# A small-h branch of h - tanh(h) rewritten: tanh times a squared arctan in place of a polynomial times tanh

## The chip, the cores and the metric

The kernel runs on one core of a Trainium2 chip. The core has a matrix engine (TensorE, "PE" in the profile), a vector engine (VectorE, DVE), a scalar engine for functions of one operand (ScalarE, ACT), a general engine (GpSimd, POOL) and a queue engine (SyncE, SP); each works through its own list of instructions in order and waits on semaphores of the others. [...] The metric is the device time of one execution in microseconds (us), as the median of several runs. Beside it stands one profiled execution with a record of every instruction.

## The reference

An attention with a decaying state (four batches, eight heads, 768 steps, 48 numbers a head), and a dense block behind it, which is what the change touches:

```python
for t in range(S):
    cur = einsum('bhd,bhe->bhde', u * k[t], v[t])
    y[t] = einsum('bhd,bhde->bhe', r[t], state + cur)
    state = w * state + einsum('bhd,bhe->bhde', k[t], v[t])
x = y.transpose(0, 2, 1, 3).reshape(3072, 384)
h = x @ w_in                 # 384 -> 2048
g = h - np.tanh(h)
out = g @ w_out              # 2048 -> 384
```

For small h the difference h - tanh(h) is about h cubed over three, and two numbers nearly alike are subtracted. So a kernel needs a second formula there, and a choice between the two for each element.

## The kernel before

**Units.** The attention is worked off in units of 64 steps of two batches. A unit loads r, k and v, transposes r and k on PE (L810), scales them on VectorE (L814, or L834 and L835 in later units), multiplies in 64 x 64 blocks (L760), writes diagonal blocks on ScalarE (L858), masks on VectorE (L993), updates the state (L951, L1002), and evicts its rows into `xt`, the input of the dense block (L924, with a part by DMA at L945).

**Weights.** The weights arrive as 64-bit numbers and are converted on the chip, in sixteen pieces of 768 columns: two steps on ScalarE (L141, L142) and five on VectorE (L139, L140, L143, L144, L145) for each piece. A dense tile can't begin before its piece is converted.

**Dense tiles.** There are 96 tiles: 256 tokens by 256 of the 2048 inner columns. For each, PE makes h in PSUM with twelve matmuls (L171). Two buffers of h take turns, so the matmuls of the tile after next wait until `s`, `th`, `tg` and `g` of this one have read it (L1053). ScalarE takes five steps (`act`, L175 to L188): `s` is the square of h, `th` is tanh h, `tg` is tanh of G1 times h, `q` is the square of (s + M1), and `small` is relu(SMALL - s), above zero where h is small. VectorE takes four (`vec`, L190 to L201): `g` = h - th; `c1` multiplies tg by C4 times s; `c2` multiplies it by (q + K1); `cp` copies tg over g where `small` isn't zero. `q` and `small` both read `s`, `c1` reads `s`, and `c2` reads `q`. The finished g goes to PE: for the first 24 tiles and for the very last as o = g times w_out, eight matmuls (L209), otherwise as seven products in place of eight (L260), for which GpSimd builds sums of g (L245 to L249) and VectorE gathers the results (L288).

**The order.** Nothing is scheduled by hand or by the framework: `lay_out` gives each step to a planner as a task with an engine, a modelled cost and the tasks that it comes after (`add`, in `hidden` from L1044 for the dense tiles). `Plan.order` works out due times backward and forward, and then tries seeded random shifts of them (`moved`), 2500 on the first 240 modelled microseconds and 500 on all, and keeps each that doesn't lengthen the modelled span. `Plan.follow` takes over the due times of the first 90 us from a plan of a simpler layout, and searches 500 times behind that. The instructions are then written out in the order of the plan. So a task that goes, or an edge that moves, alters the order of all engines. Where PE has a gap at the start, the planner puts matmuls of the identity into it (`fills`, L688). A first ACTIVATE at L726 brings ScalarE's function tables in.

Of the kernel before, what the change touches and what calls it, by code (L numbers as in the profile page):

```python
# [18 lines left out]

SMALL = 0.25
G1 = 1.0046999454498291
C4 = 0.0015550695700212612
M1, K1 = -6.776710510253906, 167.42614473500566

# [119 lines left out]
class Dense:  # L148


    def __init__(self, nc, work, gpool, ps_d, shared, out, rows, outs=None, last=None, seven=None, parts=None):
        self.nc, self.work, self.gpool, self.ps_d, self.new_outs, self.seven = nc, work, gpool, ps_d, outs, seven
        self.parts = parts
        self.out, self.rows, self.xts, self.sums, self.last, self.negative = out, rows, {}, {}, last, set()
        self.d, self.w_in_sb, self.w_out_sb, self.m1b, self.smallb = (
            shared[x] for x in ("dims", "w_in", "w_out", "m1b", "smallb"))

    def tile(self, j, fs, f):

# [14 lines left out]

    def act(self, t, x):  # L175
        A = self.nc.scalar
        out = self.tmp(x)
        setattr(t, x, out)
        if x == "s":
            A.activation(out, t.h, AF.Square)  # L180
        elif x == "th":
            A.activation(out, t.h, AF.Tanh)  # L182
        elif x == "tg":
            A.activation(out, t.h, AF.Tanh, scale=G1)  # L184
        elif x == "q":
            A.activation(out, t.s, AF.Square, bias=self.m1b)  # L186
        else:
            A.activation(out, t.s, AF.Relu, bias=self.smallb, scale=-1.0)  # L188

    def vec(self, t, x):  # L190
        V = self.nc.vector
        if x == "g":
            t.g2 = self.gpool.tile([128, 2, self.d.NT], F32, name="g", tag="g")
            t.g = t.g2.rearrange("p z t -> p (z t)")
            V.tensor_tensor(t.g, t.h, t.th, ALU.subtract)  # L195
        elif x == "c1":
            V.scalar_tensor_tensor(t.tg, t.s, C4, t.tg, ALU.mult, ALU.mult)  # L197
        elif x == "c2":
            V.scalar_tensor_tensor(t.tg, t.q, K1, t.tg, ALU.add, ALU.mult)  # L199
        else:  # L200
            V.copy_predicated(t.g, t.small.bitcast(I32), t.tg)  # L201

# [95 lines left out]
        queue.dma_start(out=self.out[runs[z] : runs[z] + size, :], in_=o[z * size : (z + 1) * size])  # L298


ACT_STEPS, VEC_STEPS = ("s", "th", "tg", "q", "small"), ("g", "c1", "c2", "cp")


class Plan:
# [243 lines left out]
def near(ctx, tc, r, k, v, w, u, out, shared, moe_w_in, moe_w_out):  # L548
# [145 lines left out]
    def lay_out(early, across_by):  # L694
# [3 lines left out]
        def add(*args, **more):  # L698
            return plan.add(*args, **more)
# [23 lines left out]
            out=ub.rearrange("p h d -> p (h d)"),  # L723
            in_=bass.AP(tensor=u.tensor, offset=u.offset, ap=[[0, 128], [1, H * D]])), data=.7)

        add("ACT", 1.3, lambda: A.activation(fixed("warm", [128, 1]), shared["one"], AF.Tanh), due=0)  # L726


        def steps(generator):
# [313 lines left out]

        def hidden(j, fs, f, due, pace, seven=False):  # L1044
            t = dense.tile(j, fs, f)
            none = SimpleNamespace(g=None, c1=None, c2=None, cp=None, o=None, h=None, s=None, q=None, small=None, th=None, tg=None, empty=[], emptied=[])
            m = len(tiles)
            plan.at = "tile", j, f
            b1, b2, b3, b5 = (tiles[m - i] if m >= i else none for i in (1, 2, 3, 5))
            x = SimpleNamespace(empty=[], emptied=[])  # L1050
            tiles.append(x)
            piece = f // 4 * 4 + f // 2 % 2
            now = add("PE", 1.29, lambda: dense.h(t, 0), filled[j, "all"] + [converted[piece], b1.h, b2.s, b2.th, b2.tg, b2.g] + ([flagged] if m == 1 else []), due, steps=12)  # L1053
            x.h = add("PE", 1.29, lambda: dense.h(t, 1), [now], due + 1.3, steps=12)
            last_h[j] = x.h
            if m == 0:
                plan.fills.append(([], now, fills(idle)))
            x.s = add("ACT", .48, lambda: dense.act(t, "s"), [x.h, b2.c1, b2.q, b2.small, b1.s])
            x.th = add("ACT", .48, lambda: dense.act(t, "th"), [x.h, b2.g, b1.th] + ([units[m].rk, units[m].kw] if m < L else []))
            x.tg = add("ACT", .48, lambda: dense.act(t, "tg"), [x.h, b2.cp, b1.tg])  # L1060
            x.q = add("ACT", .63, lambda: dense.act(t, "q"), [x.s, b2.c2, b1.q])
            x.small = add("ACT", .63, lambda: dense.act(t, "small"), [x.s, b2.cp, b1.small])
            x.g = add("DVE", .6, lambda: dense.vec(t, "g"), [x.th, x.tg, b5.o, b1.g])
            x.c1 = add("DVE", .6, lambda: dense.vec(t, "c1"), [x.s, x.tg])
            x.c2 = add("DVE", .6, lambda: dense.vec(t, "c2"), [x.q, x.c1])
            x.cp = add("DVE", .65, lambda: dense.vec(t, "cp"), [x.c2, x.small, x.g])
            if seven:

                late = j == d.NB - 1 and f >= d.NF - ALONE - LATE
                x.sg = x.cp  # L1070
                for i, cost in enumerate((.33, .2, .2) if late else (.75, .5, .5)):
                    x.sg = add("DVE" if late else "POOL", cost, lambda i=i: dense.sums_of_g(t, i), [x.sg] + ([] if i else [b3.o, b1.cp]))
                done = units[early - 1]
                now = add("PE", 1.32, lambda: dense.products(t, 0), [x.sg, mixed[f // 4], b1.o, done.cp, done.diag, done.lev] + b1.empty + b1.emptied[:2], due + 2 * pace, steps=16)
                x.o = add("PE", .99, lambda: dense.products(t, 1), [now] + b1.emptied, due + 2 * pace + 1.3, steps=12)
                if t.last:
                    finished_seven(t, x, now, due, pace)
                return
            now = add("PE", 1.3, lambda: dense.o(t, 0), [x.cp, converted[piece + 2], b1.o] + b1.empty + ([] if t.first and t.last else b1.emptied) + ([units[1].cp, units[1].diag] if m == 0 else []), due + 2 * pace, steps=8)
            if m == 0:  # L1080
                plan.fills.append(([units[1].cp, units[1].diag], now, fills(x_banks[1][:, 0])))
            x.o = add("PE", 1.3, lambda: dense.o(t, 1), [now] + b1.emptied, due + 2 * pace + 1.3, steps=8)
            if not t.last:
                return
            whole = fs[1] == d.NF
            for i in range(L):
                ends = SimpleNamespace()

                def run(i=i, ends=ends):
                    dense.empty(t, i)  # L1090
                    ends.o = t.o

                x.empty.append(add("DVE" if fs[0] or j == d.NB - 1 else "ACT", .47, run, [[now, x.o][i]] + stored.get((j - 1, i), []), due + 3 * pace))
                if whole and j < d.NB - 1:

                    stored[j, i] = [add("POOL", .6, lambda z=z, i=i, ends=ends: dense.store(ends.o, L * j + i, z, G),
                                        [x.empty[-1]], due + 4 * pace, data=.4) for z in range(2)]
# [273 lines left out]
@with_exitstack  # L1371
def kernel(
    ctx: ExitStack,
    tc: tile.TileContext,
    r: bass.AP,
    k: bass.AP,
    v: bass.AP,
    w: bass.AP,
    u: bass.AP,
    moe_w_in: bass.AP,  # L1380
    moe_w_out: bass.AP,
    out: bass.AP,
):
    nc = tc.nc
    d = Dims(r, moe_w_in)
    const = ctx.enter_context(tc.tile_pool(name="const", bufs=1))

    def fixed(name, shape, dt=F32):
        return const.tile(shape, dt, name=name, tag=name)

    ident = fixed("ident", [128, 128])
    make_identity(nc, ident)
    consts = {}
    for name, value in (("m1b", M1), ("smallb", SMALL), ("p_bias", -896.0 * 2**23), ("one", 1.0)):
        consts[name] = fixed(name, [128, 1])
        nc.vector.memset(consts[name], value)
    w_in_sb = fixed("w_in_sb", [128, d.NF // 2, d.NK, 256])
    w_out_sb = fixed("w_out_sb", [128, d.NF, d.DM])
    flag = fixed("flag", [1, 1], I32)
    last = fixed("last", [128, L, d.DM])  # L1400
    shared = {"dims": d, "ident": ident, "w_in": w_in_sb, "w_out": w_out_sb, "flag": flag, "last": last, **consts}
    with tc.manual_schedule():
        near(tc, r, k, v, w, u, out, shared, moe_w_in, moe_w_out)

    with tc.If(shared["far"] > 0):
        anywhere(tc, r, k, v, w, u, out, shared)

    for b in range(d.B):
        queue = (nc.sync, nc.scalar)[b % 2]
        queue.dma_start(out=out[(b + 1) * d.S - SHORT : (b + 1) * d.S, :],  # L1410
                        in_=shared["last"][b % 2 * SHORT : (b % 2 + 1) * SHORT, b // 2, :])
# [31 lines left out]
```

## Time and profile before

| | us |
|---|---|
| median of 3 runs | 587.53 (587.31 to 587.86) |
| span of the profiled execution | 585.9 |
| PE busy | 570.1 |
| VectorE busy | 493.5 |
| ScalarE busy | 395.6 |
| GpSimd busy | 206.1 |

The span goes from the first instruction to the last in one execution under the profiler; the runs are timed without it, and their median lies 1.6 us above. A row of a group of instructions reads: line of the kernel, engine, operation, output <- inputs, partitions x elements, count | busy us, mean ns of one | idle us of the engine just before them, and what ended it. A row of the windows reads: from:to, length, and then for each engine the busy us in that stretch and in brackets the number of instructions.

### The profile page before, as it was taken

The numbers are of one execution on the slowest core, as the hardware profiler recorded it, in microseconds if no ns is written. First come the engines' busy times: TensorE is split into PE (matmuls) and PEld (weight loads), VectorE is DVE, ScalarE is ACT, GpSimd is POOL, SyncE is SP. The second block draws the span as 40 slices with busy tenths as digits, with TensorE's granted clock in tenths as the row PEclk, the third lists the DMA queues.
The fourth block names the chain that finished last, engine by engine and source line by source line (L and its number), as shares of the span: only waits on it lengthen the run. The fifth ranks groups of instructions, "written<-read, shape, count | busy, mean of one in ns | idle before, by whom it ended". The sixth has DMA issues, their size and how long they took to land.

```text
span 585.9 us, 14391 instructions
## 1 busy us (share of the span) xinstructions
PE 570.1 (97%) x5493; PEld 481.6 (82%) x5493; DVE 493.5 (84%) x817; ACT 395.6 (68%) x893; POOL 206.1 (35%) x366
## 2 busy tenths in 40 slices
PE   8888999999999999999999999999999999999996
PEld 4566677677777699899889898989999899899995
DVE  5799969999999999977988999888877777646665
ACT  2698889979775585555575785775766765665552
POOL 6002212200000245355455465443534446354420
PEclk9999999999999999999999999999999999999999
DMA  6976986743200121232335432531223300100101
GB/s 123 216 146 123 172 201 122 159 107 80 84 0 1 20 49 28 39 56 45 52 55 90 89 57 41 96 45 32 42 43 48 57 3 8 29 8 1 27 2 31
DMA packets 138549, 38.49 MB, mean 66 GB/s; under 512 B 130760, under 2 KB 132904, under 8 KB 138472
## 3 DMA queue, kind: packets, MB, share of 16 engines
q1 hardware_dynamic: 133308, 30.30, 28.4%
q0 software_dynamic: 4992, 6.99, 5.3%
q8 instruction: 45, 0.74, 0.5%
q14 instruction: 32, 0.26, 0.2%
q10 hardware_dynamic: 172, 0.20, 0.1%
HBM read 31.66 MB, written 4.72 MB: 62 GB/s over the span
## 4 chain that ended last, share of the span: by engine, by line
PE 81%; DVE 9%; ACT 4%; issue 2%; DMA 2%; SPq 1%; POOL 0%; DVEq 0%; ACTq 0%; POOLq 0%
PE h L171 38%; PE p L260 27%; PE o L209 7%; PE yk_ps L760 6%; ACT at L858 1%; SPq L798 1%; DMA xt<-rest 1%; DVE g L201 1%; DVE tg L199 1%; PE h L688 1%; DVE g L195 1%; DVE power L144 1%; DVE at L993 1%; DMA first_k<-in_k_dram 1%; DVE tg L197 1%
## 5 line engine op out<-in xcount | busy, mean ns | idle before, releaser
L171 PE MATMUL h<-xt,w_in_sb 128*128 128x256 f32 x1152 | 281.0, 381 | 1.3 <-DVE w_in_sb L145 0.9
L171 PEld LDWEIGHTS h<-xt,w_in_sb 128*128 128x128 f32 x1152 | 213.1, 190 | 32.6 <-PE x_ps L810 1.1
L245 POOL TENSOR_TENSOR sg<-g 128x256 f32<-128x256 f32 x69 | 54.0, 783 | 224.7 <-DVE g L201 213.9
L260 PE MATMUL p<-mixed,sg 128*128 128x192 f32 x426 | 104.1, 326 | 0.0
L197 DVE SCALAR_TENSOR_TENSOR tg<-s,tg 128x512 f32<-128x512 f32 x96 | 70.2, 731 | 30.5 <-ACT tg L184 21.5
L180 ACT ACTIVATE s<-h 128x512 f32<-128x512 f32 x96 | 57.4, 597 | 54.5 <-PE h L171 54.4
L195 DVE TENSOR_TENSOR g<-h,th 128x512 f32<-128x512 f32 x96 | 65.7, 684 | 29.8 <-ACT tg L184 11.1
L182 ACT ACTIVATE th<-h 128x512 f32<-128x512 f32 x96 | 57.3, 597 | 41.7 <-PE h L171 41.7
L184 ACT ACTIVATE tg<-h 128x512 f32<-128x512 f32 x96 | 57.2, 596 | 37.8 <-PE h L171 36.2
L260 PEld LDWEIGHTS p<-mixed,sg 128*128 128x128 f32 x426 | 75.0, 190 | 0.3 <-issue 0.3
L201 DVE COPY_PREDICATED g<-small,tg 128x512 f32<-128x512 int32 x96 | 71.0, 740 | 4.0
L260 PE MATMUL p<-w_out_sb,g 128*128 128x192 f32 x284 | 71.5, 334 | 0.6 <-DVE parts L222 0.6
L209 PE MATMUL o<-w_out_sb,g 128*128 128x384 f32 x192 | 69.8, 490 | 2.1 <-DVE g L201 2.1
L199 DVE SCALAR_TENSOR_TENSOR tg<-q,tg 128x512 f32<-128x512 f32 x96 | 67.7, 705 | 4.1 <-ACT q L186 1.0
L186 ACT ACTIVATE q<-s,m1b 128x512 f32<-128x512 f32 x96 | 69.8, 727 | 0.5
L188 ACT ACTIVATE small<-s,smallb 128x512 f32<-128x512 f32 x96 | 69.6, 725 | 0.3
L260 PEld LDWEIGHTS p<-w_out_sb,g 128*128 128x128 f32 x284 | 52.1, 190 | 8.6 <-DVE parts L222 1.0
L945 POOL DMA_DIRECT2D xt<-rest x66 | 32.4, 498 | 71.4 <-ACT rest L924 71.1
L209 PEld LDWEIGHTS o<-w_out_sb,g 128*128 128x128 f32 x192 | 35.7, 190 | 19.5 <-issue 1.9
L858 ACT ACTIVATE at<-same,du 128x64 f32<-128x64 f32 x184 | 47.9, 340 | 2.0 <-DVE du L854 1.9
L249 POOL TENSOR_TENSOR sg<-sg,g 128x128 f32<-128x128 f32 x69 | 41.4, 600 | 4.9
L247 POOL TENSOR_TENSOR sg<-sg,g 128x128 f32<-128x128 f32 x69 | 40.2, 582 | 4.9
(129 smaller groups left out, 688.8 us busy)
## 6 DMA issues: line engine op xcount, KB each, us to landing
st<-in_moe_w_out_dram SPq DMA_DIRECT2D x8, 768.0 KB, 4.7
rt<-in_r_dram SPq DMA_DIRECT2D x48, 96.0 KB, 3.0
vt<-in_v_dram SPq DMA_DIRECT2D x48, 96.0 KB, 3.1
st<-in_moe_w_in_dram SPq DMA_DIRECT2D x16, 288.0 KB, 5.7
kt<-in_k_dram SPq DMA_DIRECT2D x44, 96.0 KB, 3.2
out_dram<-o POOLq DMA_DIRECT2D x44, 96.0 KB, 2.2
st<-in_moe_w_in_dram POOLq DMA_DIRECT2D x16, 96.0 KB, 5.6
parts<-in_r_dram SPq DMA_DIRECT2D x48, 32.0 KB, 2.1
```

The costliest lines, as they stand in the source:

```text
L171: self.nc.tensor.matmul(t.h2[:, z], self.w_in_sb[:, t.f // 2, kk, z * 128 : (z + 1) * 128], self.xts[t.j][:, kk].rearrange("p b t -> p (b ...
L180: A.activation(out, t.h, AF.Square)
L182: A.activation(out, t.h, AF.Tanh)
L184: A.activation(out, t.h, AF.Tanh, scale=G1)
L186: A.activation(out, t.s, AF.Square, bias=self.m1b)
L188: A.activation(out, t.s, AF.Relu, bias=self.smallb, scale=-1.0)
L195: V.tensor_tensor(t.g, t.h, t.th, ALU.subtract)
L197: V.scalar_tensor_tensor(t.tg, t.s, C4, t.tg, ALU.mult, ALU.mult)
L199: V.scalar_tensor_tensor(t.tg, t.q, K1, t.tg, ALU.add, ALU.mult)
L201: V.copy_predicated(t.g, t.small.bitcast(I32), t.tg)
L209: self.nc.tensor.matmul(self.outs[i], t.g2[:, z, i * C : (i + 1) * C], self.w_out_sb[:, t.f + z, :], start=t.first and z == 0, stop=t.last ...
L260: self.nc.tensor.matmul(ps[bank][:, half * n : (half + 1) * n], a, b, start=t.first and half == 0, stop=t.last, skip_group_check=True)
```

## The change

For small h the two factors behind the tanh, C4 s and (q + K1), are replaced by one: the square of G3 times arctan(G2 h). ScalarE makes it in two steps, `s` (now the arctan, from PSUM) and `sq` (the square, in place in SBUF). VectorE multiplies once (`m`) where it multiplied twice (`c1`, `c2`). `small` is now formed from the squared arctan, with another threshold, and so comes after `sq`. The tile `q` isn't made any more, nor the constant `m1b`; the tables' first ACTIVATE takes arctan. The planner's tasks and edges follow; its costs for the steps that stay are the same.

```diff
-SMALL = 0.25
-G1 = 1.0046999454498291
-C4 = 0.0015550695700212612
-M1, K1 = -6.776710510253906, 167.42614473500566
+G1, G2, G3 = 1.00527092, 0.30777497, 1.87096009
+SMALL = 0.05252
...
     def act(self, t, x):
         A = self.nc.scalar
+        if x == "sq":
+            A.activation(t.s, t.s, AF.Square, scale=G3)
+            return
         out = self.tmp(x)
         setattr(t, x, out)
         if x == "s":
-            A.activation(out, t.h, AF.Square)
+            A.activation(out, t.h, AF.Arctan, scale=G2)
...
-        elif x == "q":
-            A.activation(out, t.s, AF.Square, bias=self.m1b)
...
-        elif x == "c1":
-            V.scalar_tensor_tensor(t.tg, t.s, C4, t.tg, ALU.mult, ALU.mult)
-        elif x == "c2":
-            V.scalar_tensor_tensor(t.tg, t.q, K1, t.tg, ALU.add, ALU.mult)
+        elif x == "m":
+            V.tensor_tensor(t.tg, t.s, t.tg, ALU.mult)
...
-ACT_STEPS, VEC_STEPS = ("s", "th", "tg", "q", "small"), ("g", "c1", "c2", "cp")
+ACT_STEPS, VEC_STEPS = ("s", "th", "tg", "sq", "small"), ("g", "m", "cp")
...
-        add("ACT", 1.3, lambda: A.activation(fixed("warm", [128, 1]), shared["one"], AF.Tanh), due=0)
+        add("ACT", 1.3, lambda: A.activation(fixed("warm", [128, 1]), shared["one"], AF.Arctan), due=0)
...
-            x.s = add("ACT", .48, lambda: dense.act(t, "s"), [x.h, b2.c1, b2.q, b2.small, b1.s])
+            x.s = add("ACT", .48, lambda: dense.act(t, "s"), [x.h, b2.m, b2.small, b1.s])
...
-            x.q = add("ACT", .63, lambda: dense.act(t, "q"), [x.s, b2.c2, b1.q])
-            x.small = add("ACT", .63, lambda: dense.act(t, "small"), [x.s, b2.cp, b1.small])
+            x.sq = add("ACT", .63, lambda: dense.act(t, "sq"), [x.s, b1.sq])
+            x.small = add("ACT", .63, lambda: dense.act(t, "small"), [x.sq, b2.cp, b1.small])
...
-            x.c1 = add("DVE", .6, lambda: dense.vec(t, "c1"), [x.s, x.tg])
-            x.c2 = add("DVE", .6, lambda: dense.vec(t, "c2"), [x.q, x.c1])
-            x.cp = add("DVE", .65, lambda: dense.vec(t, "cp"), [x.c2, x.small, x.g])
+            x.m = add("DVE", .6, lambda: dense.vec(t, "m"), [x.sq, x.tg])
+            x.cp = add("DVE", .65, lambda: dense.vec(t, "cp"), [x.m, x.small, x.g])
...
-    for name, value in (("m1b", M1), ("smallb", SMALL), ("p_bias", -896.0 * 2**23), ("one", 1.0)):
+    for name, value in (("smallb", SMALL), ("p_bias", -896.0 * 2**23), ("one", 1.0)):
```

More of the change, by code (lines that the diff above doesn't have):

```diff
@@ L154, in __init__ @@
         self.out, self.rows, self.xts, self.sums, self.last, self.negative = out, rows, {}, {}, last, set()
-        self.d, self.w_in_sb, self.w_out_sb, self.m1b, self.smallb = (
-            shared[x] for x in ("dims", "w_in", "w_out", "m1b", "smallb"))
+        self.d, self.w_in_sb, self.w_out_sb, self.smallb = (
+            shared[x] for x in ("dims", "w_in", "w_out", "smallb"))
     def tile(self, j, fs, f):
@@ L1045, in hidden @@
             t = dense.tile(j, fs, f)
-            none = SimpleNamespace(g=None, c1=None, c2=None, cp=None, o=None, h=None, s=None, q=None, small=None, th=None, tg=None, empty=[], emptied=[])
+            none = SimpleNamespace(g=None, m=None, cp=None, o=None, h=None, s=None, sq=None, small=None, th=None, tg=None, empty=[], emptied=[])
             m = len(tiles)
```

## The prediction

> **What bounds the kernel now.** I read the page from the top: span, busy shares, then the chain of work that ended last.
>
> ```profile
> span 585.9 us, 14391 instructions
> PE 570.1 (97%) x5493; PEld 481.6 (82%) x5493; DVE 493.5 (84%) x817; ACT 395.6 (68%) x893; POOL 206.1 (35%) x366
> ...
> PE 81%; DVE 9%; ACT 4%; issue 2%; DMA 2%; SPq 1%; POOL 0%; DVEq 0%; ACTq 0%; POOLq 0%
> ```
>
> PE is busy for 570.1 of 585.9 us and makes up 81% of the chain, so whatever the other engines save, the end moves only by the time in which PE stands still or does filler work: at most 585.9 - 570.1 = 15.8 us of idling, and the fillers. VectorE's 84% is an average over stages, and so says nothing yet. The next view is the table of windows, cut where its columns change (PE, PE's weight loads, DVE, ACT, POOL, then PE's granted clock, which is full).
>
> ```profile
> 20.00:35.00 15.00, 11.98 (x241) 8.41 (x242) 12.80 (x22) 11.98 (x28) 0.00 (x0) 1.00 0.95 210
> 35.00:70.00 35.00, 32.18 (x616) 23.79 (x615) 34.63 (x64) 30.15 (x92) 8.28 (x16) 1.00 0.77 142
> 70.00:120.00 50.00, 49.01 (x797) 35.96 (x797) 45.05 (x76) 45.17 (x113) 10.89 (x22) 1.00 0.75 153
> 120.00:200.00 80.00, 80.00 (x316) 59.68 (x315) 77.79 (x124) 57.77 (x98) 4.80 (x8) 1.00 0.20 50
> 200.00:575.00 375.00, 374.31 (x3284) 339.54 (x3283) 306.68 (x501) 241.61 (x539) 172.98 (x284) 1.00 0.24 41
> 575.00:585.90 10.90, 5.99 (x28) 4.28 (x26) 5.85 (x12) 1.74 (x4) 0.00 (x0) 0.92 0.15 42
> ```
>
> Three regimes are to be seen. From 35 to 70 us VectorE is full (34.63 of 35) and PE is not: it idles 35 - 32.18 = 2.82 us. From 70 to 575 us PE is full; it idles 0.99 us, nothing and 0.69 us in the three stretches. The last 10.9 us are a tail. PE's busy time also holds matmuls that only keep its place (L688, identity into an unused bank), and the same table for that line says how much:
>
> ```profile
> 20.00:35.00 15.00, 3.44 (x7) 1.17 (x7) 1.00 0.95 210
> 35.00:70.00 35.00, 3.18 (x8) 1.28 (x8) 1.00 0.77 142
> ```
>
> So between 35 and 70 us PE has 2.82 + 3.18 = 6.0 us without useful work. What it waits for there is, by the view of waits of that window, VectorE each time, the longest of them being the first tile's finished g:
>
> ```profile
> PE o L209 <- DVE g L201: 1.6, 1, 1.6
> PE h L171 <- DVE w_in_sb L145: 0.9, 1, 0.9
> ```
>
> VectorE is the bound of that start, PE of everything behind it. The change takes work from VectorE.
>
> **The change part by part.** These are the rows of the instructions touched and of the nearest relatives of the new ones.
>
> ```profile
> L197 DVE SCALAR_TENSOR_TENSOR tg<-s,tg 128x512 f32<-128x512 f32 x96 | 70.2, 731 | 30.5 <-ACT tg L184 21.5 <-ACT s L180 7.3 <-ACT seen L886 1.7
> L199 DVE SCALAR_TENSOR_TENSOR tg<-q,tg 128x512 f32<-128x512 f32 x96 | 67.7, 705 | 4.1 <-ACT q L186 1.0
> L186 ACT ACTIVATE q<-s,m1b 128x512 f32<-128x512 f32 x96 | 69.8, 727 | 0.5
> L188 ACT ACTIVATE small<-s,smallb 128x512 f32<-128x512 f32 x96 | 69.6, 725 | 0.3
> L180 ACT ACTIVATE s<-h 128x512 f32<-128x512 f32 x96 | 57.4, 597 | 54.5 <-PE h L171 54.4
> L182 ACT ACTIVATE th<-h 128x512 f32<-128x512 f32 x96 | 57.3, 597 | 41.7 <-PE h L171 41.7
> L835 DVE TENSOR_TENSOR rT<-rT,power 128x512 f32<-128x512 f32 x12 | 8.6, 714 | 0.4
> L714 ACT COPY twice<-inverse 128x512 f32<-128x512 f32 x1 | 0.6, 622 | 3.0 <-DVE inverse L712 3.0
> ```
>
> VectorE loses c1 (731 ns) and c2 (705 ns) and gains m, a plain product of two SBUF tiles. No row shows that product itself; L835 has its form and size at 714 ns, and the scaled products bound it from 705 to 731, so the edit comes to one instruction less for each tile. In busy time that is 96 x (731 + 705 - 714) = 69 us, from 493.5 to some 424. In elapsed time an instruction counts by its pitch, start to start, on a full engine:
>
> ```profile
> 51.48 0.68 DVE L199 SCALAR_TENSOR_TENSOR tg<-q,tg 128x512 f32<-128x512 f32 x1
> 52.09 0.55 DVE L854 TENSOR_REDUCE du<-rk 128x8 f32<-128x384 f32 x1
> ```
>
> From c2 at 51.48 to the next start at 52.09 are 0.61 us. How many tiles pass while VectorE is the bound? The windows for L199 alone count c2:
>
> ```profile
> 20.00:70.00 50.00, 2.71 (x4) 1.00 0.83 162
> 70.00:120.00 50.00, 4.08 (x6) 1.00 0.75 153
> 120.00:200.00 80.00, 11.17 (x16) 1.00 0.20 50
> ```
>
> Four tiles by 70 us: 4 x 0.61 = 2.4 us that VectorE finishes earlier with the same tiles, units and converted weights, and PE has 6.0 us of empty time in that stretch to take it in. Behind it PE is full, and work that starts 2.4 us earlier ends 2.4 us earlier. The next six tiles save VectorE 3.7 us, but PE's idling there is 0.99 us: at most that much, and I take nothing, since that idling is scattered. From 120 to 575 us the saved instructions are hidden by PE's own work: 0.
>
> ScalarE: the first square becomes an arctan of the same operands with an immediate scale. Square (L180) and tanh (L182) of that form both take 597 ns, so I take 597 again; only a change of function tables could make it dearer, which is a rival below. q with its bias tile (727 ns) becomes sq, in place, with an immediate scale alone. It is bounded by 597 (same form, but from PSUM) and 727; the copy from SBUF at L714 is nearest with 622, so I take 622: 0.1 us less for each tile, 10 us of busy time, from 395.6 to some 385. In the first 70 us that is 4 x 0.1 = 0.4 us at most, on an engine that is 30.15 of 35 us busy. The new edge is that small reads sq and not s. What such an edge costs is seen where s, q and small stand in a row, since q reads s:
>
> ```profile
> 40.84 0.58 ACT L180 ACTIVATE s<-h 128x512 f32<-128x512 f32 x1
> 41.46 0.73 ACT L186 ACTIVATE q<-s,m1b 128x512 f32<-128x512 f32 x1
> 42.09 0.71 ACT L188 ACTIVATE small<-s,smallb 128x512 f32<-128x512 f32 x1
> ```
>
> q starts 0.04 us after the end of s; small, which needs nothing of q, starts 0.10 us before q's end. With the new edge small starts 0.04 us after sq's end: 0.14 us lost by each tile whose steps stand back to back, 0.6 us on four. Queued behind small on ScalarE are the units' diagonal blocks and evictions, and cp on VectorE waits for it. The 0.4 gained and the 0.6 lost I set against each other at 0, and keep both ends for the range. The memset of m1b goes (first microsecond, beside the loads), and the warm-up at L726 takes the other function: 0.
>
> The tail is read from the timeline:
>
> ```profile
> 577.42 0.73 DVE L201 COPY_PREDICATED g<-small,tg 128x512 f32<-128x512 int32 x1
> 578.04 0.34 DVE L288 TENSOR_TENSOR e<-e,p 128x192 f32<-128x192 f32 x1
> 578.44 2.85 PE L209 MATMUL p<-w_out_sb,g 128*128 128x384 f32 x8 [0.30 <-DVE e L288]
> ```
>
> The closing block of PE (eight matmuls from 578.44) waits 0.30 us for e, which stands behind cp on VectorE, and cp behind c2. With one product less, cp moves up and that wait goes: 0.3 us. Next is PE's own preceding work, so there is no more to be had.
>
> **The sum**: 2.4 + 0.3 = 2.7 us off the profiled span, 585.9 to 583.2. The median of the runs, 587.53, lies 1.6 us above this span; with the same distance the forecast is **584.8 us** (-0.46%).
>
> **A page against the trace.** That PE is full from 120 to 200 us rests on its busy time, and the pace of its matmuls confirms it. The chain has blocks there and far behind, where VectorE has room:
>
> ```profile
> 145.09 1.29 PE o L209 x4
> 146.38 1.29 PE h L171 x6
> ...
> 501.72 1.29 PE h L171 x6
> ```
>
> Six matmuls into h take 1.29 us at 146 us and 1.29 us at 501 us; four into o, with half as many columns again in each, take 1.29 us as well, the same time for a column. PE runs at one pace whether VectorE is full or not. The Trainium skill (Perfetto Trace Analysis, section Identifying the Most-Contended Engine) says that matmul busy time is a bad measure of how close one is to the peak and that the busy share of weight loads is a better one. By that page the 59.68 of 80 us of weight loads would leave PE room in this stretch; the price of that is the fourth rival. The equal paces speak against it.
>
> **The rivals.**
>
> *Hidden anyway.* The 6.0 us without useful work may not follow VectorE one for one: PE stands still or fills while first weights arrive and units go through ScalarE, which is 30.15 of 35 us busy. Against it: both waits shown name VectorE. Then only the tail is left: 587.53 - 0.3 = 587.2, between 586.4 and 588.7.
>
> *A worse order of the start.* Each engine's order is written out by a seeded random search over the list of tasks, and the list changes: one VectorE task less for each tile, other edges, the same random numbers on another list. The search can only be as good as its cost model, and its mechanism of loss is definite: one weights piece more is converted ahead of the first tiles' products (or behind them, where the products need it), while PE waits, between 35 and 70 us. A piece has five VectorE steps, three of them over 768 columns like this one:
>
> ```profile
> L144 DVE SCALAR_TENSOR_TENSOR power<-st,power 128x768 uint32<-128x768 uint32 x16 | 15.2, 951 | 0.0
> ```
>
> So it is worth between 3 x 0.95 = 2.9 and 5 x 0.95 = 4.8 us, some 4 us. One piece misplaced gives 584.8 + 4 = 588.8, two give 592.8: slower than before. It decides from 2.7 / 4, two thirds of a piece. For it speaks that VectorE has no slack in that stretch in which a wrong order could hide; against it that the model's costs for these steps (0.6 for a product) are the pitch measured.
>
> *Tables.* If arctan and tanh did not lie in one set of ScalarE's tables, each tile would switch twice. One load is in the trace:
>
> ```profile
> L726 ACT ACT_TABLE_LOAD x1 | 1.3, 1283 | 2.5 <-DVE plus L588 2.5
> ```
>
> 96 x 2 x 1.283 = 246 us on top of 395.6 make ScalarE the bound, at 642 us or more. The one load before shows that tanh, square, relu and copy share a set; of arctan no row speaks. The Trainium skill (ScalarE: Activation LUTs, section Table sets: the hidden batching unit) lists tanh and arctan together in the set that it names after sigmoid. By that page nothing switches.
>
> *PE is not full after 120 us.* Then the sixteen tiles between 120 and 200 us would each pass on 0.61 us as well: 9.8 us more, 584.8 - 9.8 = 575.0.
>
> **How the numbers follow.** The forecast's case (582.1 to 586.3, from twice the sum of 2.7 to less than half of it) has 0.57, hidden anyway 0.20, the worse order 0.19, tables 0.02, PE not full 0.02. The range takes the first case with the bound of all empty PE time (6.0 + 0.3 and 0.4 from ScalarE: 580.8) at one end and between one and two misplaced pieces at the other: 581.0 to 590.5. About 0.2%, 1.2 us, is what a measurement of this kernel can tell from no change. Faster: the forecast's case and the fourth, 0.59; same: hidden anyway, 0.20; slower: order and tables, 0.21.
>
> **What would show it.** In the profile after: VectorE's busy time near 424 us and its count 97 less (96 products, one memset); one table load; sq near 622 ns and m near 714; PE's empty time (idle and L688) between 35 and 70 us down from 6.0 to about 3.6, with PE full behind it; the wait for e at the end gone. The forecast is wrong if that empty time stays or grows, if the waits of PE in the start name ScalarE, or if PE's pace after 120 us changes.

## The result: 1.45% slower

The changed kernel takes 595.84 us as the median of 4 runs (595.79 to 597.3), the kernel before 587.69 (587.31 to 587.87): a ratio of 1.0145 with a 95% interval of 1.0131 to 1.016. The forecast was 584.8, the range ended at 590.5.

The page after, first lines, and from its groups and from the lines by group the instructions that the change touched:

```profile
span 594.0 us, 14244 instructions
PE 573.4 (97%) x5495; PEld 485.2 (82%) x5495; DVE 432.4 (73%) x720; ACT 394.5 (66%) x893; POOL 196.0 (33%) x366
...
L196 DVE TENSOR_TENSOR tg<-s,tg 128x512 f32<-128x512 f32 x96 | 68.7, 716 | 10.9 <-ACT s L176 7.6
...
L176 ACT ACTIVATE s<-s 128x512 f32<-128x512 f32 x96 | 61.1, 637 | 0.8
...
L723 ACT ACT_TABLE_LOAD x1 | 1.3, 1283 | 2.5 <-DVE plus L585 2.5
```

Every instruction costs nearly what was estimated: the product 716 ns (714 forecast), the square in place 637 (622), one table load, 97 VectorE instructions fewer. VectorE is busy 61 us less. And the span is 8.0 us longer. The windows of the changed kernel, cut as before, say where:

```profile
20.00:35.00 15.00, 12.34 (x175) 7.98 (x175) 9.44 (x16) 7.55 (x19) 0.00 (x0) 0.89 1.03 207
35.00:70.00 35.00, 29.34 (x604) 22.03 (x604) 33.11 (x58) 29.76 (x88) 5.59 (x11) 1.00 0.55 103
70.00:120.00 50.00, 47.52 (x845) 36.09 (x846) 39.75 (x67) 39.71 (x110) 11.87 (x24) 0.93 0.79 150
120.00:200.00 80.00, 80.00 (x313) 59.00 (x312) 76.40 (x121) 65.47 (x120) 4.66 (x9) 1.00 0.37 82
200.00:575.00 375.00, 373.85 (x3271) 338.03 (x3270) 253.52 (x418) 238.28 (x525) 164.39 (x287) 1.00 0.23 39
```

From 120 us on PE is as full as before, but it has more left to do there: it is busy for 468.17 us behind 120 us, where it was 460.30. So 7.9 of the 8.0 us are lost ahead of that. Two columns show it: PE idles more (5.66 us from 35 to 70, where it was 2.82; 2.48 from 70 to 120, where it was 0.99), and the granted clock is below 1 in two stretches where it was full.

Two places make most of it, and the units show how much each is worth. The table has the start, in us, of a unit's products for the state (`yk_ps<-vt,kw` in PE's timeline), and below it the lag:

| unit | 1st | 2nd | 9th | 10th | 12th | span |
|---|---|---|---|---|---|---|
| before | 15.23 | 23.84 | 83.43 | 92.00 | 106.99 | 585.93 |
| changed | 15.71 | 28.43 | 87.77 | 100.84 | 115.31 | 593.98 |
| lag | 0.5 | 4.6 | 4.3 | 8.8 | 8.3 | 8.0 |

The lag comes ahead of the second unit and between the ninth and the tenth, and stays. The first place, in the timeline of PE, for the kernel before and then for the changed one (start, length, what, and in brackets the idle time ahead and what ended it):

```profile
17.95 1.55 PE L688 MATMUL h<-ident 128*128 128x512 f32 x3
20.91 1.55 PE L688 MATMUL h<-ident 128*128 128x512 f32 x3 [1.41 <-issue]
22.40 0.58 PE L760 MATMUL yk_ps<-at,vt 64*64 64x64 f32 x24
```

```profile
17.23 1.55 PE L685 MATMUL h<-ident 128*128 128x512 f32 x3
22.64 4.42 PE L685 MATMUL h<-ident 128*128 128x512 f32 x7 [3.86 <-issue]
26.99 0.58 PE L757 MATMUL yk_ps<-at,vt 64*64 64x64 f32 x24
```

The second unit's output products start at 26.99 us and not at 22.40: PE stands still for 3.86 us ahead of fillers, waiting for nothing that the profile shows (the last section comes back to this), and then works off seven records of fillers at a lowered clock. The second place, around 92 us of the changed kernel, in PE's timeline, VectorE's, and the windows (the column behind POOL is the clock):

```profile
94.30 1.13 PE L757 MATMUL yk_ps<-rT,state 48*64 48x64 f32 x32 [2.29 <-DVE rT L811]
...
96.22 2.93 PE L169 MATMUL h<-xt,w_in_sb 128*128 128x256 f32 x6
...
101.94 1.46 PE L169 MATMUL h<-xt,w_in_sb 128*128 128x256 f32 x6
```

```profile
90.73 0.69 DVE L196 TENSOR_TENSOR tg<-s,tg 128x512 f32<-128x512 f32 x1 [0.35 <-ACT s L176]
...
93.47 0.68 DVE L811 TENSOR_TENSOR rT<-x_ps,power 128x512 f32<-128x512 f32 x1
```

```profile
92.00:94.00 2.00, 0.01 (x1) 0.00 (x0) 2.00 (x4) 1.89 (x8) 0.00 (x0) 1.00 1.04 397
94.00:96.00 2.00, 1.70 (x64) 1.73 (x64) 1.97 (x5) 0.87 (x2) 0.00 (x0) 0.53 1.19 228
96.00:98.00 2.00, 2.00 (x16) 1.61 (x9) 1.41 (x3) 1.45 (x2) 0.00 (x0) 0.50 0.14 28
98.00:100.00 2.00, 2.00 (x11) 1.30 (x12) 1.31 (x2) 0.00 (x0) 0.00 (x0) 0.50 0.58 111
```

A unit's scaled r (L811) stands on VectorE behind steps of a tile, one of which waits for the new square; PE idles 2.29 us, and then has half its clock for some 7 us: six matmuls into h take 2.93 us, not 1.46. The busy columns hide that, for a slow PE is a busy PE.

### The profile page after: what moved, and what is told of

Read it like the earlier page. It is cut to its first block, busy times and chain, and to the rows that moved or that the text cites. A ratio compares the mean times of both kernels' runs of the same rounds, so it can differ in the third digit from the quotient of the medians.

```text
span 594.0 us, 14244 instructions
## 1 busy us (share of the span) xinstructions
PE 573.4 (97%) x5495; PEld 485.2 (82%) x5495; DVE 432.4 (73%) x720; ACT 394.5 (66%) x893; POOL 196.0 (33%) x366
## 4 chain that ended last, share of the span: by engine, by line
PE 85%; DMA 4%; SPq 3%; ACT 3%; DVE 2%; issue 1%; DVEq 0%; ACTq 0%
PE h L169 41%; PE p L257 27%; PE o L206 9%; PE yk_ps L757 6%; SPq L795 3%; DMA kt<-in_k_dram 2%; DMA st<-in_moe_w_out_dram 1%; PE x_ps L807 1%; DMA st<-in_moe_w_in_dram 1%; ACT at L855 1%; PE x_ps L757 0%; DVE rT L811 0%; PE p L206 0%; DMA rt<-in_r_dram 0%; DVE tg L196 0%
## 5 line engine op out<-in xcount | busy, mean ns | idle before, releaser
L242 POOL TENSOR_TENSOR sg<-g 128x256 f32<-128x256 f32 x69 | 51.9, 752 | 230.0 <-DVE g L198 201.4
L196 DVE TENSOR_TENSOR tg<-s,tg 128x512 f32<-128x512 f32 x96 | 68.7, 716 | 10.9 <-ACT s L176 7.6
L176 ACT ACTIVATE s<-s 128x512 f32<-128x512 f32 x96 | 61.1, 637 | 0.8
L244 POOL TENSOR_TENSOR sg<-sg,g 128x128 f32<-128x128 f32 x69 | 36.4, 528 | 4.7
L246 POOL TENSOR_TENSOR sg<-sg,g 128x128 f32<-128x128 f32 x69 | 36.4, 527 | 4.7
L257 PE MATMUL p<-mixed,g 128*128 128x192 f32 x142 | 34.7, 326 | 0.0
```

Source lines behind the costliest of these rows:

```text
L176: A.activation(t.s, t.s, AF.Square, scale=G3)
L196: V.tensor_tensor(t.tg, t.s, t.tg, ALU.mult)
L257: self.nc.tensor.matmul(ps[bank][:, half * n : (half + 1) * n], a, b, start=t.first and half == 0, stop=t.last, skip_group_check=True)
```

## The experiments

Theory A: the instructions are as cheap as thought, and the order that the planner's search found for the new list loses the time. Theory B: the new instructions, above all the edge from `sq` to `small` and the product, lose it in any order. All ratios are to the kernel before, run beside each experiment (medians 587.88 to 588.23), with 95% intervals; they are the ratios on record, and not exactly the quotients of the medians.

**The new arithmetic in the old order.**

```diff
+            pair = iter(("sq", "small"))
-            x.sq = add("ACT", .63, lambda: dense.act(t, "sq"), [x.s, b1.sq])
-            x.small = add("ACT", .63, lambda: dense.act(t, "small"), [x.sq, b2.cp, b1.small])
+            x.q = add("ACT", .63, lambda: dense.act(t, next(pair)), [x.s, b2.c2, b1.q])
+            x.small = add("ACT", .63, lambda: dense.act(t, next(pair)), [x.s, b2.cp, b1.small])
...
-            x.m = add("DVE", .6, lambda: dense.vec(t, "m"), [x.sq, x.tg])
-            x.cp = add("DVE", .65, lambda: dense.vec(t, "cp"), [x.m, x.small, x.g])
+            x.c1 = add("DVE", .6, lambda: None, [x.s, x.tg])
+            x.c2 = add("DVE", .6, lambda: dense.vec(t, "m"), [x.q, x.c1])
+            x.cp = add("DVE", .65, lambda: dense.vec(t, "cp"), [x.c2, x.small, x.g])
```

> The new arithmetic written out in the order of the kernel before: the planner gets the old task list (s, th, tg, q, small, g, c1, c2, cp with their old edges and costs), but s is the arctan, the first of the two slots q and small to come squares in place and the second makes small, the slot of c1 issues nothing and the slot of c2 the one product. Theory A (the order alone was lost, the instructions are cheaper): between 584.0 and 587.5 us, PE empty from 35 to 70 us by at most the 6.0 us of before. Theory B (the new instructions or the new edge from sq to small cost the time, whatever the order): 592 us or more, with PE waiting on ScalarE's s and small in the start.

586.51 us, ratio 0.9972 (0.9957 to 0.9987). The new arithmetic in the old order makes the kernel slightly faster, within theory A's range and with its 5.8 us of empty PE time (2.63 idle, 3.18 filler); theory B is out as the cause of the 8 us. But the gain isn't where the prediction put it. The windows of this run:

```profile
35.00:70.00 35.00, 32.37 (x615) 23.99 (x616) 33.00 (x61) 30.45 (x92) 8.10 (x16) 1.00 0.76 141
70.00:120.00 50.00, 48.91 (x798) 36.13 (x796) 42.20 (x70) 45.34 (x114) 10.75 (x22) 1.00 0.79 156
120.00:200.00 80.00, 80.00 (x316) 59.68 (x315) 69.56 (x108) 57.80 (x99) 4.57 (x8) 1.00 0.20 50
```

VectorE is busy 33.00 us from 35 to 70 us, not 34.63, so 1.6 us are freed; PE does 615 matmuls there, where it did 616. VectorE waits instead, for ScalarE's copies of the units' transposed k (`kT`). These are all waits of VectorE that the profile shows from 35 to 70 us, in the kernel before and then in this run (us in total, times, longest):

```profile
DVE rT L814 <- ACT kT L846: 0.2, 1, 0.2
```

```profile
DVE rT L811 <- ACT kT L843: 1.8, 3, 0.8
```

The 1.6 us went into these waits. The new product waits for the square as well, but only behind 120 us, where VectorE has room.

How far PE has got can be read at equal matmuls, as its order is the same in both. It starts the 13th tile's h at 126.79 us (126.76 before), the last matmul into h at 572.31 (573.21), and the span ends at 584.58 (585.93). So the two are level at 127 us; 0.9 us are gained from there to 573 us, where the prediction had nothing, and 0.5 in the tail. These are single profiled executions, and this one began 0.9 us late: VectorE waited 1.21 us for a load of weights (at 20.80 us), ahead of any tile, and PE started the first tile's h at 28.95 us (28.06 before).

**The old arithmetic in the new order.**

```diff
-            x.sq = add("ACT", .63, lambda: dense.act(t, "sq"), [x.s, b1.sq])
+            x.sq = add("ACT", .63, lambda: dense.act(t, "q"), [x.s, b1.sq])
-            x.m = add("DVE", .6, lambda: dense.vec(t, "m"), [x.sq, x.tg])
+            x.m = add("DVE", .6, lambda: (dense.vec(t, "c1"), dense.vec(t, "c2")), [x.sq, x.tg])
```

> The old arithmetic in the order of the changed kernel: the planner gets the new task list, but sq makes q, and the slot of m issues c1 and c2 one behind the other. Theory A: 595.8 us or more, since the order is the slow one and VectorE has 0.61 us more for each tile: 596 to 599. Theory B: back to near 587.7, at most 590.

617.57 us, ratio 1.0517 (1.0483 to 1.0551). Slower than the changed kernel, as theory A has it, but by 22 us where up to 3 were expected. The plan had reserved one VectorE step where this run issues two, and PE idles behind 120 us as well. So the run shows that this order has no room for the extra instruction; it doesn't show how slow the order by itself is for the old arithmetic:

```profile
120.00:200.00 80.00, 74.23 (x279) 51.73 (x278) 78.03 (x121) 62.59 (x114) 4.34 (x9) 1.00 0.37 85
200.00:575.00 375.00, 364.49 (x3201) 326.04 (x3200) 295.96 (x481) 231.17 (x512) 158.93 (x271) 1.00 0.22 38
```

**Other seeds.** In both searches, and in both kernels:

```diff
-        return self.listed(self.search(pinned(due), tries, Random(5), until))
+        return self.listed(self.search(pinned(due), tries, Random(6), until))
...
-        chance, until = Random(5), self.BUSY
+        chance, until = Random(6), self.BUSY
```

> The changed kernel with another seed (6 for 5) in both random searches of the planner. Theory A (the order that one seed finds is a draw from a spread of some us): a time that differs from 595.8 by more than 2 us, with the loss at other places of the start. Theory C (the new task list makes every order slow): 594 to 598, PE empty in the same two places.

> The kernel before with seed 6 in both searches. Theory A: also off 587.7 by more than 2 us, more likely slower, up to 596. Theory C: within 2 us of 587.7, since the old list is planned well with any seed.

> The changed kernel with seed 7. If the order is a draw: anywhere from 585 to 597, with the time following how much of PE's time up to 120 us is empty, filler or at half clock. If the changed list is bad as such: 592 to 597, slower than the kernel before with the same seed by 4 us or more.

> The kernel before with seed 7. Draw: 587 to 597, the difference to the changed kernel of the same seed of either sign. If the old list is good as such: within 2 us of 588.

> The changed kernel with seed 8. As for seed 7: 585 to 597 for a draw, 592 to 597 if the list is bad as such.

> The kernel before with seed 8. As for seed 7: 587 to 597 for a draw, near 588 if the old list is good as such.

| seed | old list, us (ratio, interval) | new list, us (ratio, interval) |
|---|---|---|
| 5 | 587.69 (1) | 595.84 (1.0145, 1.0131 to 1.0160) |
| 6 | 592.74 (1.0091, 1.0068 to 1.0114) | 592.74 (1.0076, 1.0059 to 1.0092) |
| 7 | 596.02 (1.0139, 1.0116 to 1.0162) | 597.05 (1.0150, 1.0133 to 1.0167) |
| 8 | 595.95 (1.0133, 1.0112 to 1.0154) | 589.55 (1.0022, 1.0008 to 1.0037) |

Four seeds spread each list over 7 to 8 us. The means, 593.1 for the old list and 593.8 for the new, lie 0.7 us apart, and the difference at one seed goes from +8.2 to -6.4 us. With four draws of such a spread the means can't tell lists apart that differ by 1 or 2 us. The kernel before is the best draw of its four; the changed one is the third of its four. The expectation that the old list is planned well with any seed fell, and so did the one that the new list is bad as such, by the times.

The times follow PE's empty time only loosely: with seed 8 the new list has 18.5 us of idle and filler time from 20 to 120 us and a span of 590.3 us, the old list 16.6 and 593.8. And the first place may not be a mere draw: the second unit's products for the state start at 28.4, 29.1, 29.5 and 27.5 us in the four new orders and at 23.8, 23.0, 26.6 and 27.2 in the four old ones. So part of the loss sits at one place in each, where other places were expected. Why was not tested.

**Without the fillers at the first place.**

```diff
             free, runs = fitted.get(t.n, (0.0, [])) if t.engine == "PE" else (0.0, [])
+            if t.key[0] == ("unit", 1) and 18 < t.start < 24:
+                runs = []
```

> The changed kernel without the filler matmuls that stand in PE's list right ahead of the second unit's output products (ten records in the profile, 17.2 to 27.0 us). Nothing else is altered, and the order is the same. Theory A1 (the start slipped since PE stood still for 3.9 us and then worked off seven fillers at a lowered clock while the unit's products were ready): those products start near 22.7 us and not at 26.99, and the time falls by 2 to 4.5 us, to 591.3 to 594. Theory A2 (the slip comes from loads and ScalarE's list, and the fillers only fill a hole): within 1 us of 595.8.

592.07 us, ratio 1.0064 (1.0045 to 1.0082): 3.8 us less than the changed kernel by the medians, 2.6 by the profiled spans (591.4 against 594.0). The products are let go earlier, but PE stops within them, with nothing shown that it waits for. At the second place the wait is shorter, and the clock stays up:

```profile
21.73 0.47 PE L759 MATMUL yk_ps<-at,vt 64*64 64x64 f32 x2 [3.52 <-DVE at L992]
24.25 0.81 PE L759 MATMUL yk_ps<-at,vt 64*64 64x64 f32 x20 [2.04 <-issue]
...
92.97 0.69 PE L759 MATMUL yk_ps<-rT,state 48*64 48x64 f32 x32 [1.82 <-DVE rT L813]
...
94.12 1.56 PE L169 MATMUL h<-xt,w_in_sb 128*128 128x256 f32 x6
```

So both places count. In this run the units lag behind the kernel before by 2.9 us at the second unit (26.78) and 3.0 at the ninth (86.44), then by 6.3 at the tenth (98.31) and 5.8 at the twelfth (112.79), and the span by 5.5. Without these fillers the first place still costs 2.9 us, 1.4 of them there already at the first unit (16.63), and the second 3.3, where six matmuls into h take 1.56 us at the full clock and not 2.93. What is left at the two places no run took apart.

The same edit on the new arithmetic in the old order:

> The new arithmetic in the old order (as e1) without the fillers at the same place (here six records). A1: the second unit's products start at 21 us and not near 22.6, and the time falls from 586.5 by 1 to 1.5 us, to about 585. A2: within 0.7 us of 586.5. A colder clock could also cost up to 1 us.

586.14 us, ratio 0.9974 (0.9961 to 0.9988), the same as with the fillers, as A2 had it. But the products did start earlier, as A1 had it, and the gain was gone by the first tile's h. With the fillers, and then without (timeline of PE, and the window with the clock):

```profile
21.31 0.58 PE L757 MATMUL yk_ps<-at,vt 64*64 64x64 f32 x24
28.95 2.83 PE L169 MATMUL h<-xt,w_in_sb 128*128 128x256 f32 x12 [0.17 <-PE x_ps L757]
...
20.00:35.00 15.00, 11.54 (x239) 7.87 (x239) 12.20 (x19) 11.32 (x27) 0.00 (x0) 1.00 0.99 206
```

```profile
19.89 0.58 PE L759 MATMUL yk_ps<-at,vt 64*64 64x64 f32 x24 [2.09 <-DVE at L992]
29.39 2.86 PE L169 MATMUL h<-xt,w_in_sb 128*128 128x256 f32 x12
...
20.00:35.00 15.00, 12.37 (x236) 8.93 (x236) 12.25 (x20) 11.33 (x27) 0.00 (x0) 0.77 1.00 211
```

Without the fillers the granted clock falls to 0.77 of full in this window; with them it stays full. So here the fillers cost 1.4 us ahead of the products and keep the clock behind them, and the time is the same either way.

**More and fewer VectorE instructions in the old order.** First with a second instruction behind the product, then with no product:

```diff
-            x.c2 = add("DVE", .6, lambda: dense.vec(t, "m"), [x.q, x.c1])
+            x.c2 = add("DVE", .6, lambda: (dense.vec(t, "m"), V.tensor_tensor(t.tg, t.tg, t.tg, ALU.max)), [x.q, x.c1])
...
+            x.c2 = add("DVE", .6, lambda: None, [x.q, x.c1])
```

> As e1, but with one VectorE instruction more for each tile behind the product, the maximum of tg with itself, so that VectorE has as many instructions as before the change. If VectorE's instructions bound the start, as the prediction had it, 586.5 goes up by 2.4 us or more, to 589 or above. If the start is bound by the units' chain through all engines, it stays within 1 us of 587.5.

593.6 us, ratio 1.0097 (1.008 to 1.0114): 7.1 us more than with one product, what VectorE as the bound called for. But the number of instructions alone doesn't set this price: the kernel before has as many on VectorE, in the same order, and takes 5.4 us less. There the first of the two, `c1`, has a slot of its own ahead; here both stand in the slot of `c2`, behind the square. No run put the extra instruction into the slot of `c1`.

> As e1, but the product is left out (small elements get the plain tanh), so VectorE has two instructions for each tile less than before the change, and cp waits for small alone. VectorE as the bound: another 2 to 3 us less than e1, 583.5 to 584.5, with PE's progress at 70 us ahead by that. Units' chain as the bound: within 1 us of 586.5, and PE's empty time from 35 to 70 us as before.

585.41 us, ratio 0.9957 (0.994 to 0.9974): 1.1 us less than with one product, between what the two theories called for, and not clear of the run with one product, as the intervals overlap. This kernel leaves out the correction for small h, so it serves for the time alone. From 35 to 70 us VectorE now has 3.7 us less to do than in the kernel before, and PE gets 0.6 us of it; most of the rest goes into the same waits for ScalarE:

```profile
35.00:70.00 35.00, 32.78 (x617) 24.11 (x617) 30.92 (x56) 30.42 (x94) 8.15 (x16) 1.00 0.79 144
...
DVE rT L811 <- ACT kT L843: 3.3, 4, 1.3
DVE state L948 <- ACT rest L921: 0.5, 1, 0.5
```

In one and the same order an instruction more for each tile, at that place, costs 7.1 us; one less gives 1.1, not clear of noise. VectorE being 99% busy in that stretch meant that it had no room there, not that taking away would help.

## Why the prediction was wrong

*Durations and busy times*: right. Product and square came within 15 ns. VectorE fell to 432.4 us where 424 were forecast, ScalarE to 394.5 where 385 were. The durations added up did fall as forecast on VectorE, by 96 x (731 + 705 - 716) = 69 us; but a busy time counts an overlap of two instructions once, and it fell by 61, so the steps overlap less than before.

*Tables*: right, one load. The section on table sets of the Trainium skill (ScalarE: Activation LUTs) agrees with the trace.

*PE full from 120 us*: right by the columns; 80.00 of 80 us again, and the rival that PE is not full, with its 0.02, fell. The term of nothing from 120 to 575 us was too small all the same: in the old order the new arithmetic gained 0.9 us there, with PE idle 0.36 us from 200 to 575 where it was 0.69; the columns don't show the rest.

*The tail*: the wait for e at the end did go. The last block of PE follows the one ahead without a gap (timeline of the changed kernel); 0.3 us were forecast, and in the old order it was 0.5.

```profile
586.25 0.49 PE L257 MATMUL p<-w_out_sb,sg 128*128 128x192 f32 x2
586.58 2.74 PE L206 MATMUL p<-w_out_sb,g 128*128 128x384 f32 x8
```

*"Four tiles by 70 us: 4 x 0.61 = 2.4 us that VectorE finishes earlier with the same tiles, units and converted weights, and PE has 6.0 us of empty time in that stretch to take it in."* This is the step that failed, twice. First, it took the order as given, while the change has every list written anew. In the new lists PE's empty time from 35 to 70 us, idle and filler (L685), is 5.66 + 2.64 = 8.3 us; 3.6 were forecast.

```profile
35.00:70.00 35.00, 2.64 (x7) 0.98 (x6) 1.00 0.55 103
```

Second, even in the old order the step doesn't hold. With one instruction less for each tile PE is level with the kernel before at 127 us, or 0.9 us ahead if the late start of that execution is taken off, where 2.4 us were forecast; with two less it gains 0.6 us from 35 to 70 us. What came in its place are VectorE's waits for ScalarE's copies of the units, 0.2 us before, 1.8 with one instruction less and 3.3 with two: VectorE can't finish earlier than the units let it. That a full engine bounds its stretch was inferred from its busy share and from which engine PE waited for; both are also what one sees where a chain of units goes in turn through PE, VectorE and ScalarE and the list has packed VectorE to fit. That in the old order this chain holds VectorE up is shown by these waits; that it alone sets PE's pace up to 120 us is argued. In the changed kernel the longest wait of PE from 35 to 70 us names ScalarE, one of the prediction's own signs of being wrong:

```profile
PE yk_ps L757 <- ACT s L181: 2.0, 1, 2.0
```

So that the old order's gain, 1.4 us by the spans, is still half of the 2.7 us forecast is luck: 0.9 of it comes from a stretch that was put at nothing. The rival *hidden anyway*, with its 0.20, had the mechanism of the old order's start: it names the units that go through ScalarE.

*The rival of a worse order*: the right case in kind, with 0.19 too small and priced too low. It was one misplaced weights piece, 4 us, and two at most 592.8. In fact the draws go from 587.7 to 597.1 us for the two lists. A piece does come late in the changed kernel, the second of `w_in`, converted at 43.3 us where it was 34.5. But from 35 to 70 us PE waits 0.3 us for weights, less than the 0.9 of before, and the units' lag doesn't grow there. What costs time in this order are fillers ahead of the units' products, a pause of PE and half the clock after a gap. What makes the other draws slow was not taken apart. Nothing in one profile of one order could show that spread. What could have been seen is that the order was one draw of a search; then the fair forecast is the middle of the draws, plus the small gain.

## What to carry to other kernels

Where a search or a planner writes the order, a change of the task list is two changes. Measure it with the order held, and over several seeds, before crediting or blaming the arithmetic; here the held order gave -0.28% and the redrawn one +1.45%. And an engine at 99% in a packed stretch says little of what a removal gives: try the removal of one and of two instructions, and see in the waits what the freed time turns into, before promising either. The version worth keeping is the new arithmetic in the old order, 586.51 us, or the best of several seeds.

## What the runs showed of the hardware

PE's granted clock fell to half after a gap of 2.29 us (94.30 us above) and stayed there for some 7 us; after a gap of 1.82 us at the same place it did not. The Trainium skill (TensorE: Matmul & The Clock Gate, section Why this matters for your kernels) says that PE keeps its clock where no gap between bursts is longer than about 3 us. Here 2.29 us were enough, with only small matmuls (64 columns) behind the gap; the measurement decides. The length alone doesn't decide either: with two instructions in the slot of `c2` a gap of 2.28 us (up to 46.74 us) left the clock full, and in the new list with seed 7 one of 1.86 us (up to 57.63 us) was followed by half the clock for 3.4 us. No run here varies the gap alone. That fillers can keep the clock is shown by the pair of windows above, 1.00 with them and 0.77 without, in one order.

PE also stood still 3.86 us, 1.41 us and 2.04 us between 18 and 25 us in three kernels, with nothing shown that it waited for, in the middle of a block of like products in one of them. The place is the same in PE's list each time. The windows from the start to just ahead of the end of the pause, for the kernel before, the changed one and the changed one without the fillers, count 219 or 220 matmuls and 220 weight loads (the first two columns):

```profile
0.00:20.90 20.90, 16.69 (x220) 9.98 (x220) 11.61 (x27) 7.58 (x23) 9.17 (x37) 1.00 0.81 135
0.00:22.63 22.63, 16.07 (x220) 9.68 (x220) 11.44 (x26) 9.08 (x24) 9.49 (x37) 1.00 0.86 139
0.00:24.24 24.24, 15.98 (x219) 10.09 (x220) 13.56 (x29) 8.96 (x24) 9.07 (x37) 0.93 0.88 144
```

Thirteen of the fourteen kernels have such a pause at that count, of 0.8 to 6.1 us, whatever instruction stands there; the fourteenth, the old order without the fillers, shows none. In each of the thirteen the trace has a packet of 16 KB on an instruction queue (q8) that lands 1.5 to 2.3 us before PE goes on (18.75 to 20.38 us in the changed kernel, where PE goes on at 22.64). So PE seems to wait there for its next instructions. No run varied their delivery, so this is argued and not shown.
